# Attention's last value sums in a bank of the scores, and the first MLP unit with its high weights' products first

## The chip, the cores and the metric

The kernel runs on one core of a Trainium2 chip. The metric is the device time of one execution in microseconds (us). TensorE (PE) multiplies and accumulates into the eight banks of PSUM, VectorE (DVE) and ScalarE (ACT) read PSUM and work on SBUF, GpSimd (POOL) works on SBUF alone, and the queue of SyncE (SP) issues the transfers. PEld in the rows is PE's load of the stationary operand, which runs beside its matmuls.

## What is computed

A masked attention over 2 batches, 8 heads, 768 positions and 64 channels is followed by two MLPs over the 1536 tokens. The mask lets a query see the keys with its own hash bucket.

```python
scores = scale * np.matmul(q, k.transpose(0, 1, 3, 2))
scores = np.where(mask, scores, -1000000000.0)
attn = np.exp(scores - np.max(scores, axis=-1, keepdims=True))
attn = attn / (np.sum(attn, axis=-1, keepdims=True) + 1e-09)
x = np.matmul(attn, v)                       # then (1536, 512)

g = x @ w_gate                               # 512 x 1536
x = (g * sigmoid(g) * (x @ w_val)) @ w_out   # 1536 x 512

h = x @ w_in                                 # 512 x 1024
solu = h * softmax(h)
out = (layernorm(solu) * g_ln) @ w_out2      # 1024 x 512
```

## The kernel before

Each number is split into a high and a low part of reduced precision, and each product of two is done as three matmuls: high by high, high by low, low by high. The high part is a cast, the low part a subtraction.

**Attention** goes by slots: 128 queries of one head against its 768 keys. Three slots make a quarter, and a pair of heads has four. For each slot PE writes the scores `s` (two buffers of two PSUM banks, pool `ps_s`), DVE takes the maxima, ACT the exponentials, PE turns them (`transposes`, L535), ACT casts the high part `eh` (L544) and DVE subtracts the low part `el` (L548). `values` (L551 on) then multiplies a whole quarter's `eh` and `el` with the values, in three parts of four matmuls, and adds them up in one PSUM tile `av` of 128 x 384; its pool `ps_a` has one buffer, bank 6. `results` (L602 on) takes `av` out. For the last two quarters it does so without a transfer: ACT copies the lower half of the tile (L624), DVE adds the upper half to it (L626), and only then may the next quarter's `values` overwrite the bank. `spread` (L593 on) turns the reciprocals of the row sums with three PE transposes into the tile `pp` (pool `ps_p`, one buffer), and DVE multiplies the result `xf` by it (L649; for the last quarter L629). POOL, or ACT and DVE for the last quarter, then split `xf` into `xh` and `xl`.

**The first MLP** goes by units. A unit (`hidden`, L930 on) takes 128 of the 1536 hidden columns and 512 tokens: 12 matmuls give the gate `h0` and 12 the value `h1`. Their pool `ps_h` has two buffers for each, and takes over the four banks of `ps_s`: the first `h0` lies in bank 0, the first half of the scores' first buffer, and the first `h1` in bank 2. Then come Silu on ACT (L945), the product on DVE (L946) and the split (L948, L951). Three units share one set of weights.

**Weights** come as 64-bit numbers. DVE turns each piece into 32-bit floats in six steps (`to_float32`, L47 to L64), one ACT cast and one DVE subtraction split it (L913, L915). The first unit's weights are ready as floats before; ACT casts their high part (L841) and POOL subtracts the low part (L842).

**The order** on each engine is fixed when the program is built. Inside each of the two stages it is the code's. Where the stages meet, a scheduler with a cost model interleaves the rows of both: it put two matmuls of the first MLP unit ahead of the last quarter's `values`, and others between its parts.

Of the kernel before, what the change touches and what calls it, by code (L numbers as in the profile page):

```python
# [9 lines left out]
F32 = mybir.dt.float32  # L10
# [10 lines left out]
P = 128  # L21
# [46 lines left out]
def hash_attention_then_two_mlps(  # L68
# [16 lines left out]
    nc = tc.nc  # L85
# [6 lines left out]
    HALF = S // 2  # L92
    CH = C // 2
    NP = H // 2
    KD = DM // P
    KF = DFF // P
    KF2 = DFF2 // P
    BLK = 512
# [12 lines left out]
    xh = xpool.tile([P, KD, NT], R32, tag="h", name="xh")  # L111
    xl = xpool.tile([P, KD, NT], R32, tag="l", name="xl")
# [93 lines left out]
    with at:  # L206
# [4 lines left out]
        ps_s = at.enter_context(tc.tile_pool(name="ps_s", bufs=2, space=PSUM))  # L211
# [246 lines left out]
        for top in tops:  # L458
            nc.vector.memset(top, 1.0)
        s_of, nm_of, e_of, t_of, eh_of, el_of, av_of, total_of, r_of, rs_of, x_of = (  # L460
            {} for _ in range(11)
        )
        NQ = NSLOT // CH

        def quarter(h):


            p, l = divmod(h, 4)
            return (p, l // 2, l % 2) if p == 0 else (p, l % 2, l // 2)
# [83 lines left out]
        def values(h, part):  # L553


            if not 0 <= h < NQ:
                return
            p, j, n = quarter(h)
            if part == 0:
                av_of[h] = ps_a.tile([P, HALF], F32, tag="av", name="av")  # L560
            av = av_of[h]
            vj = parts[p, "v"][:, j].rearrange("p c t d -> p c (t d)")
            for c in range(2 * part, 2 * part + 2):
                low = (av[0:D], vj[:, c, 0:D], el_of[h][:, c, :])
                if c == C - 1:
                    nc.tensor.matmul(*low, start=False, stop=False)
                nc.tensor.matmul(  # L567
                    av, vj[:, c], eh_of[h][:, c, :], start=c == 0, stop=c == C - 1
                )
                if c < C - 1:  # L570
                    nc.tensor.matmul(*low, start=False, stop=False)  # L571
# [171 lines left out]
        with tc.manual_schedule():  # L743
# [7 lines left out]
            for i in range(NSLOT + 9):  # L751
                p, l = divmod(i, SLOTS)
                h, part = divmod(i - 5, CH)
# [25 lines left out]
                if part == 2 and h == NQ - 1:  # L779
                    spread(*quarter(h)[::2])  # L780
                values(h, part)
                go(work)
                if i == 2:
# [30 lines left out]
    with ExitStack() as m1:  # L814
        def pool(name, bufs, **kw):
            return m1.enter_context(
                tc.tile_pool(name=name, bufs=bufs, reuse_waits="tile", **kw)
            )
# [4 lines left out]
        ps_h = pool("ps_h", 2, space=PSUM)  # L823
# [10 lines left out]
        def weights1(f):  # L834
            hi, lo = halves(ws)
            w1_of[f] = [x.rearrange("p n (k f) -> p n k f", k=KD) for x in (hi, lo)]
            return hi, lo

        hi, lo = weights1(0)
# [89 lines left out]

        def hidden(f, blk):  # L930
            hi, lo = w1_of[f]
            ps = []
            for n in range(2):
                p = ps_h.tile([P, BLK], F32, tag=f"h{n}", name=f"h{n}")
                for kk in range(KD):
                    for a, x in ((hi, xh), (hi, xl), (lo, xh)):
                        nc.tensor.matmul(  # L937
                            p, a[:, n, kk, :], x[:, kk, blk * BLK:(blk + 1) * BLK],
                            start=kk == 0 and a is hi and x is xh,
                            stop=kk == KD - 1 and a is lo,  # L940
                        )
                ps.append(p)
            yield
            sg = sg_.tile([P, BLK], F32, tag="sg", name="sg")
            nc.scalar.activation(sg, ps[0], AF.Silu)  # L945
            nc.vector.tensor_mul(sg, ps[1], sg)  # L946
            ah = ap_.tile([P, BLK], R32, tag="ah", name="ah")
            nc.scalar.copy(ah, sg)  # L948
            yield
            al = ap_.tile([P, BLK], R32, tag="al", name="al")  # L950
            nc.vector.tensor_sub(al, sg, ah.bitcast(F32))  # L951
            act[f, blk] = ah, al
# [38 lines left out]
        with tc.manual_schedule():  # L991
# [5 lines left out]
            for t in range(TH):  # L997
                for unit in range((FT + 1) * NBLK):
                    f, blk = divmod(unit, NBLK)
                    reached = (t, unit)  # L1000
                    if t == TH - 1 and unit == FT * NBLK:

                        yh = xpool.tile([P, KD, NT], R32, tag="h", name="yh")
                        yl = xpool.tile([P, KD, NT], R32, tag="l", name="yl")
                    work = hidden(t * FT + f, blk) if f < FT else summed(t, blk)
                    go(work)
                    if f < FT:

                        go(stream)
                        go(before)  # L1010
                        for _ in range(3):
                            if next(stream, None) == "copied":
                                break
                        go(work)
                        before = work
                        continue

                    go(before)
                    before = lows(blk - 1) if t == TH - 1 and blk else iter(())
                    for d in range(KD):  # L1020
                        if blk and t == TH - 1:
                            go(before)
                        elif d != 1:
                            go(stream)
                        go(work)
    with ExitStack() as m2:
# [7 lines left out]
        ps_h = pool("ps_h2", 2, space=PSUM)  # L1034
# [135 lines left out]
```

## Time and profile before

| | us |
|---|---|
| median of 3 runs (lowest, highest) | 703.41 (701.28, 703.53) |
| the profiled execution's own time | 704.01 |
| its span, from the first to the last instruction | 702.2 |
| PE busy in the span | 692.0 |
| DVE busy | 557.0 |
| ACT busy | 339.3 |
| POOL busy | 150.6 |

Times in the rows count from the start of the span. The rows of one engine's timeline show start, duration, line, tiles and shape; in square brackets stands the idle time before a row and what ended it. A matmul's duration is longer than the time until the next can start, so how fast PE goes is read from the distance between starts.

### The profile page before, as it was taken

How to read it: one execution, taken by the hardware profiler on the slowest of the kernel's cores; microseconds unless marked ns; L12 is line 12 of the kernel's file. 1: busy time of each engine (PE TensorE's matmuls, PEld its weight loads, DVE VectorE, ACT ScalarE, POOL GpSimd, SP SyncE). 2: the span in 40 equal slices, each digit the busy share in tenths (PEclk: the TensorE clock that was granted, in tenths of full speed). 3: DMA queues.
4: the chain of work that ended last, by engine and by line, in shares of the span. 5: the costliest groups of instructions: out<-in, count | busy, mean ns of one | idle time of the engine just before them, and what ended most of it. 6: DMA issues, size and time to landing. Idle time of an engine off the chain costs nothing.

```text
span 702.2 us, 10083 instructions
## 1 busy us (share of the span) xinstructions
PE 692.0 (99%) x3683; PEld 592.8 (84%) x3683; DVE 557.0 (79%) x974; ACT 339.3 (48%) x676; POOL 150.6 (21%) x156
## 2 busy tenths in 40 slices
PE   8999999999999999999999999999999999999997
PEld 5899999999999978888888888888888888888886
DVE  6799999999989988767786887977988886655461
ACT  4888989889898954432213122032133522222222
POOL 7346666556634260000000000000000000000000
PEclk7899999999999999999999999999999999999999
DMA  7654746547161403231323131131321000000001
GB/s 209 150 137 126 177 114 161 127 116 176 39 156 43 134 12 120 65 116 61 106 74 118 62 119 62 60 121 60 91 95 56 1 15 16 31 15 16 31 15 46
DMA packets 36177, 60.59 MB, mean 86 GB/s; under 512 B 4984, under 2 KB 26552, under 8 KB 35616
## 3 DMA queue, kind: packets, MB, share of 16 engines
q1 hardware_dynamic: 36128, 59.95, 29.6%
q8 instruction: 29, 0.48, 0.3%
q14 instruction: 20, 0.16, 0.1%
HBM read 36.71 MB, written 3.15 MB: 57 GB/s over the span
## 4 chain that ended last, share of the span: by engine, by line
PE 93%; DVE 2%; issue 2%; ACT 2%; DMA 1%; POOL 0%; SPq 0%; ACTq 0%; POOLq 0%; DVEq 0%
PE h L937 28%; PE h L1050 10%; PE s L484 9%; PE t L535 8%; PE y L963 5%; PE y L964 5%; PE y L962 5%; PE av L567 4%; PE av L571 4%; PE o L1101 3%; PE o L1103 3%; PE o L1102 3%; PE pp L443 2%; PE pp L405 2%; PE t L1088 1%
## 5 line engine op out<-in xcount | busy, mean ns | idle before, releaser
L937 PE MATMUL h<-xh,hi 128*128 128x512 f32 x288 | 112.2, 389 | 0.1
L937 PE MATMUL h<-xl,hi 128*128 128x512 f32 x288 | 112.1, 389 | 0.0
L937 PE MATMUL h<-xh,lo 128*128 128x512 f32 x288 | 112.1, 389 | 0.0
L548 DVE TENSOR_TENSOR el<-t,eh 128x384 fp32r<-128x384 f32 x192 | 97.8, 550 | 9.2 <-ACT eh L544 6.8
L520 ACT ACTIVATE e<-s,nm 128x768 f32<-128x768 f32 x96 | 97.8, 1019 | 5.9 <-DVE nm L504 2.7
L1076 POOL TENSOR_TENSOR w<-w,half 128x1 f32<-128x1 f32 x12 | 6.6, 551 | 416.2 <-DVE w L1075 311.0
L544 ACT CAST eh<-t 128x384 fp32r<-128x384 f32 x192 | 84.1, 494 | 21.8 <-PE t L535 20.5
L495 DVE TENSOR_REDUCE top<-s 128x1 f32<-128x768 f32 x96 | 90.6, 944 | 3.7 <-PE s L484 3.5
L535 PE MATMUL t<-idr,e 128*128 128x128 f32 x576 | 81.0, 276 | 0.4 <-DVE el L548 0.3
L535 PEld LDWEIGHTS t<-idr,e 128*128 128x128 f32 x576 | 68.5, 141 | 9.7 <-DVE el L548 4.0
L567 PE MATMUL av<-eh,vs 128*128 128x384 f32 x192 | 66.2, 345 | 1.4 <-DVE xf L626 1.4
L937 PEld LDWEIGHTS h<-xh,hi 128*128 128x128 f32 x288 | 54.1, 188 | 11.5 <-ACT hi L841 0.3
L937 PEld LDWEIGHTS h<-xl,hi 128*128 128x128 f32 x288 | 54.1, 188 | 11.3
L937 PEld LDWEIGHTS h<-xh,lo 128*128 128x128 f32 x288 | 54.1, 188 | 11.1
L948 ACT CAST ah<-sg 128x512 fp32r<-128x512 f32 x36 | 22.4, 623 | 74.7 <-DVE sg L946 74.7
L484 PE MATMUL s<-ka,qa 128*128 128x384 f32 x192 | 56.5, 376 | 0.0
L963 PE MATMUL y<-al,hi 128*128 128x512 f32 x144 | 56.1, 389 | 0.0
L962 PE MATMUL y<-ah,hi 128*128 128x512 f32 x144 | 56.1, 389 | 0.0
L964 PE MATMUL y<-ah,lo 128*128 128x512 f32 x144 | 56.0, 389 | 0.0
L946 DVE TENSOR_TENSOR sg<-h,sg 128x512 f32<-128x512 f32 x36 | 24.8, 689 | 37.7 <-PE h L937 22.1
L571 PE MATMUL av<-el,vs 128*64 128x384 f32 x160 | 54.0, 338 | 0.0
L913 ACT CAST hi<-wf 128x1024 fp32r<-128x1024 f32 x17 | 17.9, 1050 | 69.8 <-DVE wf L64 69.8
(195 smaller groups left out, 1427.3 us busy)
## 6 DMA issues: line engine op xcount, KB each, us to landing
raw<-in_moe_w_out_dram SPq DMA_DIRECT2D x10, 1024.0 KB
raw<-in_moe_w_gate_dram SPq DMA_DIRECT2D x12, 512.0 KB
raw<-in_moe_w_val_dram SPq DMA_DIRECT2D x12, 512.0 KB
ka<-kt SPq DMA_DIRECT2D x30, 192.0 KB
raw<-in_moe_w_in_dram SPq DMA_DIRECT2D x4, 1024.0 KB
v<-in_v_dram SPq DMA_DIRECT2D x8, 384.0 KB
kb<-kt SPq DMA_DIRECT2D x15, 192.0 KB
qb<-qa SPq DMA_DIRECT2D x15, 192.0 KB
```

Of the source, the lines that this page charges most:

```text
L484: nc.tensor.matmul(s[:, n, :HALF], a[:, rows], m[:, n * HALF:(n + 1) * HALF], start=first, stop=not first,)
L495: nc.vector.tensor_reduce(top[:, 1:2], s_of[i][:, :, :HALF], AX.XY, ALU.max, negate=True)
L520: nc.scalar.activation(e, s_of.pop(i)[:, :, :HALF], AF.Exp, bias=nm[:, 1:2], scale=nm[:, 0:1], accum_out=total_of[p, n][:, j, c:c + 1],)
L535: nc.tensor.transpose(t[:, m, :], e_of[i][:, g, m * P:(m + 1) * P], idf)
L544: nc.scalar.copy(half_tile(eh_of, i, g), t_of[i, g])
L548: last_of[i] = nc.vector.tensor_sub(half_tile(el_of, i, g), t_of.pop((i, g)), half_tile(eh_of, i, g).bitcast(F32),)
L567: nc.tensor.matmul(av, vj[:, c], eh_of[h][:, c, :], start=c == 0, stop=c == C - 1)
L571: nc.tensor.matmul(*low, start=False, stop=False)
L937: nc.tensor.matmul(p, a[:, n, kk, :], x[:, kk, blk * BLK:(blk + 1) * BLK], start=kk == 0 and a is hi and x is xh, stop=kk == KD - 1 and a ...
L962: nc.tensor.matmul(p, hi[:, cols], ah, start=f == t * FT, stop=False)
L963: nc.tensor.matmul(p, hi[:, cols], al, start=False, stop=False)
L964: nc.tensor.matmul(p, lo[:, cols], ah, start=False, stop=f == (t + 1) * FT - 1)
```

## The change

`values` takes the tile of the last quarter (h = NQ - 1) from the scores' pool `ps_s` and uses the first 384 columns of its first bank. By the alternation of the two buffers that is bank 0. All other quarters stay in `ps_a`. Nothing else in `values` or `results` is touched; `results` copies and adds from the tile that it is given.

`hidden` writes its 24 matmuls from a list. For the very first unit the list is sorted so that the 16 products with high weights (`hi` by `xh` and by `xl`, first for `h0`, then for `h1`) stand ahead of the 8 with low weights. All other units keep their order. Number, shape and operands of all instructions are the same.

```diff
@@ values
-            if part == 0:
+            if part == 0 and h == NQ - 1:
+                av_of[h] = ps_s.tile([P, 2, 512], F32, tag="s", name="s")[:, 0, :HALF]
+            elif part == 0:
                 av_of[h] = ps_a.tile([P, HALF], F32, tag="av", name="av")
@@ hidden
-            ps = []
-            for n in range(2):
-                p = ps_h.tile([P, BLK], F32, tag=f"h{n}", name=f"h{n}")
-                for kk in range(KD):
-                    for a, x in ((hi, xh), (hi, xl), (lo, xh)):
-                        nc.tensor.matmul(
-                            p, a[:, n, kk, :], x[:, kk, blk * BLK:(blk + 1) * BLK],
...
+            ps = [ps_h.tile([P, BLK], F32, tag=f"h{n}", name=f"h{n}") for n in range(2)]
+            order = [
+                (n, kk, a, x)
+                for n in range(2) for kk in range(KD)
+                for a, x in ((hi, xh), (hi, xl), (lo, xh))
+            ]
+            if f == blk == 0:
+                order.sort(key=lambda o: o[2] is lo)
+            for n, kk, a, x in order:
+                nc.tensor.matmul(
+                    ps[n], a[:, n, kk, :], x[:, kk, blk * BLK:(blk + 1) * BLK],
...
```

The scheduler orders the seam between the stages anew. On PE, before, from the first `spread` of the seam on (`pp_3884` is its tile, `av_3888` the last quarter's, `h0_3988` the first unit's):

```order
L600 MATMUL pp_3884<-idr_95,wide_3857 128x128 [waits Pool_49]
L600 MATMUL pp_3884<-idr_95,wide_3857 128x128 x2
L937 MATMUL h0_3988<-xh_61,hi1_3973 128x512 [waits Activation_49]
L937 MATMUL h0_3988<-xl_62,hi1_3973 128x512
L567 MATMUL av_3888<-eh_3820,vs_3440 128x384 [waits DVE_49]
L571 MATMUL av_3888<-el_3821,vs_3440 64x384
```

The wait for DVE is the one for L626 of the quarter before, which reads the one bank of `av`. Six more `values` rows follow, then ten rows of `h0` and two of `h1`, the second `spread` with the last four `values`, and the rest of the unit. The same place on PE in the changed program, up to the first row of the unit (lines from 560 on stand 3 higher, the unit's matmul at L945; `s_3888` is the last quarter's tile):

```order
L603 MATMUL pp_3884<-idr_95,wide_3857 128x128 x2
L570 MATMUL s_3888<-eh_3820,vs_3440 128x384 [waits Activation_49]
L574 MATMUL s_3888<-el_3821,vs_3440 64x384 [waits DVE_49]
...
L603 MATMUL pp_3903<-idr_95,wide_3894 128x128 [waits DVE_49,Pool_49]
L603 MATMUL pp_3903<-idr_95,wide_3894 128x128 x2
L570 MATMUL s_3888<-eh_3820,vs_3440 128x384
L574 MATMUL s_3888<-el_3821,vs_3440 64x384
L569 MATMUL s_3888<-el_3821,vs_3440 64x384
L570 MATMUL s_3888<-eh_3820,vs_3440 128x384
L945 MATMUL h0_3988<-xh_61,hi1_3973 128x512 [waits DVE_49]
```

Left out are six more `values` rows. All twelve `values` matmuls and the second `spread` now stand ahead of the whole unit, and the unit's first row waits for DVE. On DVE, before, the rows from the two that follow the second last quarter on (`xf_3880<-av_3888` reads the last quarter):

```order
L626 TENSOR_TENSOR xf_3880<-av_3834,low_3881 64x384 [waits Activation_49]
L649 TENSOR_TENSOR xf_3721<-xf_3721,pp_3884 128x384 [waits DMAHW7_49,PE_49,Pool_49]
L53 TENSOR_SCALAR wf_3986<-wf_3986 128x1024 [waits DVE_49]
L57 SCALAR_TENSOR_TENSOR wf_3986<-raw_3981,wf_3986 128x1024 [waits DVE_49]
L62 TENSOR_SCALAR raw_3981<-raw_3981 128x1024 [waits DVE_49]
L626 TENSOR_TENSOR xf_3880<-av_3888,low_3881 64x384 [waits Activation_49]
L629 TENSOR_TENSOR xf_3880<-xf_3880,pp_3903 128x384 [waits DVE_49]
```

And in the changed program (`s_3888` in the place of `av_3888`):

```order
L629 TENSOR_TENSOR xf_3880<-av_3834,low_3881 64x384 [waits Activation_49]
L652 TENSOR_TENSOR xf_3721<-xf_3721,pp_3884 128x384 [waits DMAHW7_49,PE_49,Pool_49]
L53 TENSOR_SCALAR wf_3986<-wf_3986 128x1024 [waits DVE_49]
L57 SCALAR_TENSOR_TENSOR wf_3986<-raw_3981,wf_3986 128x1024 [waits DVE_49]
L629 TENSOR_TENSOR xf_3880<-s_3888,low_3881 64x384 [waits Activation_49]
L62 TENSOR_SCALAR raw_3981<-raw_3981 128x1024 [waits DVE_49]
```

The last quarter's addition moved one place up, from behind L62 to behind L57. On ACT the cast of `xh` (L630) moved ahead of the Silu's table load. POOL's order is the same. Around the end of the first MLP a few rows of PE, DVE and ACT trade places, and on SP the small transfer of `g_ln` goes ahead of one weight transfer.

## Rows read from the trace of the kernel before

**Rows 1.** Page, part 1: busy us, share of the span, instructions.

```profile
PE 692.0 (99%) x3683; PEld 592.8 (84%) x3683; DVE 557.0 (79%) x974; ACT 339.3 (48%) x676; POOL 150.6 (21%) x156
```

**Rows 2.** Busy us and instructions of each engine in stretches, with the granted clock.

```profile
core 0: us, PE busy (x) PEld busy (x) DVE busy (x) ACT busy (x) POOL busy (x), PEclk, DMA share, GB/s
...
255.00:257.00 2.00, 0.58 (x4) 0.29 (x3) 1.97 (x4) 0.47 (x1) 2.00 (x3) 1.00 0.00 0
...
265.00:600.00 335.00, 335.00 (x1487) 276.99 (x1486) 267.11 (x375) 94.02 (x143) 2.22 (x4) 1.00 0.22 74
```

**Rows 3.** Timeline of PE where the stages meet.

```profile
start us, us, engine line op out<-in xcount [idle before <-releaser]
...
253.97 0.49 PE L600 MATMUL pp<-idr,wide 128*128 128x128 f32 x3
254.52 0.50 PE L937 MATMUL h<-xh,hi 128*128 128x512 f32 x1
254.86 0.40 PE L937 MATMUL h<-xl,hi 128*128 128x512 f32 x1
256.67 0.44 PE L567 MATMUL av<-eh,vs 128*128 128x384 f32 x1 [1.42 <-DVE xf L626]
...
258.18 0.39 PE L937 MATMUL h<-xh,lo 128*128 128x512 f32 x1
...
260.93 0.49 PE L600 MATMUL pp<-idr,wide 128*128 128x128 f32 x3
261.18 0.42 PE L567 MATMUL av<-eh,vs 128*128 128x384 f32 x1
...
261.79 0.34 PE L567 MATMUL av<-eh,vs 128*128 128x384 f32 x1
261.96 0.40 PE L937 MATMUL h<-xh,lo 128*128 128x512 f32 x1
...
264.27 0.39 PE L937 MATMUL h<-xh,hi 128*128 128x512 f32 x1
```

**Rows 4.** Timeline of DVE in the same stretch.

```profile
253.66 0.98 DVE L548 TENSOR_TENSOR el<-t,eh 128x384 fp32r<-128x384 f32 x2
...
256.07 0.54 DVE L626 TENSOR_TENSOR xf<-av,low 64x384 f32<-64x384 f32 x1
256.54 0.53 DVE L649 TENSOR_TENSOR xf<-xf,pp 128x384 f32<-128x384 f32 x1
257.00 1.30 DVE L53 TENSOR_SCALAR wf<-wf 128x1024 int32<-128x1024 int32 x1
258.34 2.20 DVE L57 SCALAR_TENSOR_TENSOR wf<-raw,wf 128x1024 int32<-128x1024 int32 x1
...
262.67 0.55 DVE L626 TENSOR_TENSOR xf<-av,low 64x384 f32<-64x384 f32 x1 [0.89 <-ACT low L624]
```

**Rows 5.** Timeline of ACT: the copy of the last quarter.

```profile
262.16 0.47 ACT L624 COPY low<-av 64x384 f32<-64x384 f32 x1 [6.67 <-PE av L567]
```

**Rows 6.** Timeline of POOL in the same stretch.

```profile
254.59 1.92 POOL L589 TENSOR_TENSOR wide<-one,r 128x192 f32<-128x192 f32 x2 [1.10 <-PE pp L600]
256.48 2.98 POOL L842 TENSOR_TENSOR lo<-w1f,hi 128x512 fp32r<-128x512 f32 x2
259.43 1.80 POOL L652 TENSOR_TENSOR xh<-xf,one 128x384 fp32r<-128x384 f32 x1
```

**Rows 7.** Stretches again: early ones in which the granted clock changed.

```profile
5.00:8.00 3.00, 1.97 (x13) 1.30 (x12) 1.28 (x2) 2.79 (x4) 2.78 (x11) 1.00 0.70 191
8.00:9.00 1.00, 1.00 (x3) 0.58 (x3) 0.00 (x0) 0.97 (x3) 0.94 (x1) 0.57 1.04 386
9.00:21.00 12.00, 11.06 (x39) 8.11 (x38) 8.04 (x10) 4.01 (x10) 11.56 (x9) 0.50 0.73 209
21.00:22.00 1.00, 1.00 (x6) 1.00 (x5) 0.96 (x3) 0.84 (x3) 0.00 (x0) 0.60 0.11 15
```

**Rows 8.** Timeline of PE: 512-column matmuls early on, and the ones behind them.

```profile
6.12 0.47 PE L355 MATMUL pp<-kt,hash_k 128*128 128x512 f32 x1 [0.48 <-ACT kt L321]
6.42 0.28 PE L355 MATMUL av<-kt,hash_k 128*128 128x256 f32 x1
7.24 0.49 PE L355 MATMUL pp<-kt,hash_first 64*128 64x512 f32 x1 [0.54 <-POOL hash_first L193]
...
14.88 0.80 PE L355 MATMUL pp<-kt,hash_k 128*128 128x512 f32 x1 [0.94 <-DVE qb L379]
15.48 0.43 PE L355 MATMUL av<-kt,hash_k 128*128 128x256 f32 x1
```

**Rows 9.** Two DVE lines over the whole span: duration ns min/median/max, first and last start.

```profile
L53 DVE TENSOR_SCALAR wf<-wf x25: 679/693/1304, 257.0 to 544.8; 128x1024 int32<-128x1024 int32 x25
...
L57 DVE SCALAR_TENSOR_TENSOR wf<-raw,wf x25: 1209/1217/2201, 258.3 to 546.6; 128x1024 int32<-128x1024 int32 x25
```

More of the change, by code (lines that the diff above doesn't have):

```diff
@@ L931, in hidden @@
             hi, lo = w1_of[f]
-            ps = []
-            for n in range(2):
-                p = ps_h.tile([P, BLK], F32, tag=f"h{n}", name=f"h{n}")
-                for kk in range(KD):
-                    for a, x in ((hi, xh), (hi, xl), (lo, xh)):
-                        nc.tensor.matmul(
-                            p, a[:, n, kk, :], x[:, kk, blk * BLK:(blk + 1) * BLK],
[L939 to L942, printed above, removed]
+            ps = [ps_h.tile([P, BLK], F32, tag=f"h{n}", name=f"h{n}") for n in range(2)]
[9 more added lines that the diff above has]
+                    ps[n], a[:, n, kk, :], x[:, kk, blk * BLK:(blk + 1) * BLK],
+                    start=kk == 0 and a is hi and x is xh,
+                    stop=kk == KD - 1 and a is lo,
+                )
             yield
```

## The prediction, made before the run

> **What bounds the kernel now.** I read the shares first: PE is busy for 692.0 of 702.2 us [rows 1], so only what lets PE idle, or slows it, can move the time. Next come the stretches, of which two matter [rows 2]. From 265 to 600 us PE is busy for 335.00 of 335 us: whatever time the seam between attention and the first MLP gains or loses is carried to the end, since nothing behind it waits that could absorb it, and the other engines' work there hangs on PE's own units and moves with them. From 255 to 257 us PE is busy for only 0.58 of 2 us: that is the seam. The timeline of PE shows the gap [rows 3]: after two matmuls of the first MLP unit the next row, the first of the last quarter's values, starts at 256.67 after 1.42 us of idle time, released by L626 on DVE, which reads the quarter before out of the single `av` bank.
>
> **The wait that is removed.** With a bank of its own the last quarter needs only its operands. The first spread starts at 253.97, and a spread holds PE for 0.25 (260.93 to 261.18 [rows 3]), so its values start at 254.22. Their last `el` is being made from 253.66, two pieces in 0.98 us [rows 4]; the first piece is there at about 254.2, the second at 254.64, and the second is wanted only by the eighth matmul. Eight value matmuls take 258.18 - 256.67 = 1.51 us [rows 3], so they are done at 255.73. Before, the same point was reached at 258.18, with two unit matmuls done in between (254.52 to 255.09, if the second takes 0.23).
>
> **What is late next.** Two waits, both on DVE, which the old order had hidden.
>
> First, the second spread writes the one `pp` buffer and so waits for L649, which ends at 256.54 + 0.53 = 257.07 [rows 4]. The step from DVE's end to PE's start took 256.67 - (256.07 + 0.54) = 0.06 us [rows 3, 4]. So the spread starts at 257.13, and PE idles from 255.73: 1.40 us. Before, the spread came at 260.93 and waited for nothing. POOL's `wide`, which it also needs, is there at 254.59 + 1.92 = 256.51 [rows 6], in time.
>
> Second, spread and four value matmuls take 261.96 - 260.93 = 1.03 us, so PE is through with attention at 258.16; the last value matmul starts 0.86 us into that (261.79), at 257.99. The unit's first row must then wait, because `h0` lies in the same bank 0: ACT's copy starts 0.37 us after the start of that matmul (261.79 to 262.16 [rows 3, 5]), at 258.36, and is done at 258.83. DVE, however, is not free. Its addition L626 stands behind L53 and L57 in the new order, and L57 ends at 258.34 + 2.20 = 260.54 [rows 4]. None of these DVE and POOL rows waits for anything that the change moves, so I take their times as they stand. L626 starts a little before its forerunner's end (L649 did by 0.07), at 260.47, takes 0.54 and lets PE go at 261.07. It takes no longer beside POOL: it took 0.54 with POOL at work (256.07) and 0.55 with POOL nearly done (262.67). PE idles from 258.16 to 261.07: 2.91 us.
>
> **The unit itself.** From 261.07 PE does 24 matmuls. After a wait the first holds PE for 0.34 (254.52 to 254.86), and ten of the same kind took 264.27 - 261.96 = 2.31, or 0.23 each [rows 3]; together 0.34 + 23 x 0.23 = 5.63, so the second unit starts at 266.70. Before it started at 264.27. **The seam costs 2.4 us at full clock.** The two parts of it agree: idle time of 1.40 + 2.91 = 4.31 us in place of 1.58 (255.09 to 256.67) and 0.30 (254.22 to 254.52). The sorting of the high weights' products costs and gains nothing: it was to keep PE from waiting for POOL's low weights, but L842 ends at 256.48 + 2.98 = 259.46 [rows 6], before the unit can begin at all. Its bounds are 0 and 0.
>
> The rest I cost at nothing. The table load on ACT moves behind the `xh` cast, but Silu needs `h0`, which comes later than both. The rows that trade places at the end of the first MLP lie where PE never waited (335.00 of 335), with the same DVE work in front. The `g_ln` transfer goes in front of a weight transfer that is wanted many units later. If one of these covers were gone, a DVE step of 1.2 us (L57's median [rows 9]) would be the likely price; the range has room for it.
>
> **The clock.** The trace shows that PE's clock can fall in a thin stretch. From 5 to 8 us PE was busy for 1.97 of 3 us, with gaps of 0.48 and 0.54; then the granted clock fell from 1.00 to 0.50 (2.4 to 1.2 GHz) and stayed there past 21 us [rows 7, 8]. In the gap at 255 us, 0.58 busy of 2, it stayed at 1.00 [rows 2]. The new seam is thinner than either: from 255.73 to 261.07, 5.3 us, PE works for 1.03. I take it that the clock falls. What it costs then: at the lower level a 512-column matmul holds PE twice as long (14.88 to 15.48 against 6.12 to 6.42: 0.60 and 0.30 [rows 8]), so half of the time that the unit's stream spends there is lost. How long a dense stream stays there no row shows. One end is 0. The other is the longest that PE worked without a pause before the clock came back, from 14.88 to within 21 to 22 us, at most 6.7 us (60% mean clock in that slice puts the rise at 21.8), a loss of 3.4; with the pauses, from 8 us on, it was 13 us, a loss of 6.5, but in that stretch PE was held up again and again. The unit's stream has no pauses, so I go by the nearer row and take the middle of 0 and 3.4: 1.7 us.
>
> The Trainium skill, page "TensorE: Matmul & The Clock Gate", section "Why this matters for your kernels", warns of PE idle gaps between bursts of matmuls from a certain length on; each of the two gaps worked out here is shorter. By that rule the clock would stay, and the time would be that of the first rival below. The fall at 8 us, after gaps that are shorter still, is why I give it the smaller chance.
>
> **The sum.** 2.4 + 1.7 = 4.1 us. Against the profiled execution's own 704.01 us (span 702.2) that gives 708.1; the median of the three runs is 0.6 lower, 703.41, and against it I forecast **707.5 us**.
>
> **The rivals.**
>
> - The clock stays up: the seam costs its 2.4 us alone, 705.8. For it: the clock stood through 1.42 us of idle time. Against it: two gaps close together, the second twice that long.
> - DVE is not held up, and the time is not slower beyond what can be told: this one ends on the other side. L53 and L57 took 1.30 and 2.20 us where their medians over 25 are 0.69 and 1.22 [rows 4, 9], with POOL at work beside them [rows 6]. If that did not come back, L57 would end at 257.00 + 0.69 + 0.04 + 1.22 = 258.95, L626 at 259.4, the unit would start at 259.5 and the seam would cost 0.8 us: 704.2, with too short a gap for the clock to fall. The balance point is 258.6: a unit that starts by then costs nothing. Against it: POOL's rows are the same in the new order, and nothing releases them later.
> - The bank does not bind: the unit starts right behind the values at 258.16, and 5.63 us later the second unit at 263.79, 0.5 us earlier than before: 702.9. The order speaks against it, since the unit's first row has a wait for DVE. Even so it would be a gain too small to tell.
>
> **How the numbers follow.** This kernel's measurement can tell about 0.3%, or 2.1 us, from no change. Forecast (clock falls) 0.64, clock stays 0.22, DVE free 0.08, bank free 0.03, anything else 0.03. The forecast's own range goes from 2.4 + 0.5 to 2.4 + 3.4 us, 706.3 to 709.2. For 8 in 10 I reach down into the rival of the clock, with 1 us for the spread of the runs (701.28 to 703.53 for one kernel): 704.6 to 709.4. Slower by over 0.3%: nearly all of the forecast and a little over half of the clock's rival, whose 2.4 us lie close to the bound, 0.76. Within: 0.21. Faster: 0.03.
>
> **What would show it.** In the profile of the changed kernel: no wait ahead of the first value matmul at about 254.2; an idle time of about 1.2 to 1.4 us ahead of the second spread, ended by DVE's product (L652 there); one of about 2.7 to 2.9 us ahead of the unit's first row at about 261, ended by DVE's addition (L629 there), with L57 at about 2.2 us just before it; a granted clock under 1.00 somewhere from 259 to 268 us and starts of the unit's matmuls some 0.43 us apart there; from then on PE busy without a gap up to 600 us. If the unit starts before 260, the DVE step is wrong; if the clock stays at 1.00, its step is; if PE idles anywhere from 270 to 600, the view that the rest just moves along is.

## The result, and the profile after

The changed kernel is slower by about half a per cent: a median of 707.5 us (705.76 to 709.47, 6 runs) against 703.77 us (701.28 to 705.11, 6 runs) of the kernel before, a ratio of 1.0055 with a 95% interval of 1.0032 to 1.0078. Its profiled execution took 705.76 us, with a span of 704.0.

The page's first part of the changed kernel answers to [rows 1]: busy us, share of the span, instructions.

```profile
PE 689.7 (98%) x3683; PEld 590.3 (84%) x3683; DVE 554.9 (79%) x974; ACT 339.9 (48%) x676; POOL 150.6 (21%) x156
```

The instruction counts are the same to the last one; PE's busy time is even 2.3 us less. That comes from ahead of the place that the change touches: up to the first spread of the seam PE is busy for 245.7 us, and for 249.5 in the kernel before. The stretches show a clock that differs there (busy us and count of each engine, granted clock, DMA share, GB/s; compare [rows 2, 7]):

```profile
core 0: us, PE busy (x) PEld busy (x) DVE busy (x) ACT busy (x) POOL busy (x), PEclk, DMA share, GB/s
...
9.00:21.00 12.00, 10.63 (x60) 7.59 (x60) 10.49 (x18) 7.73 (x18) 11.62 (x9) 1.00 0.71 213
...
255.00:259.00 4.00, 1.37 (x8) 1.00 (x9) 3.90 (x5) 0.48 (x1) 3.92 (x4) 0.99 0.00 0
259.00:262.00 3.00, 3.00 (x8) 2.33 (x9) 1.54 (x3) 1.79 (x2) 1.40 (x1) 0.50 0.00 0
...
266.00:600.00 334.00, 334.00 (x1483) 276.01 (x1482) 265.57 (x368) 94.13 (x143) 2.23 (x4) 1.00 0.22 74
```

Three things are to be seen here. From 9 to 21 us the granted clock is 1.00, where it was 0.50 in the execution of before that was profiled [rows 7]. From 255 to 259 us PE is busy for 1.37 of 4 us, and from 259 to 262 us the granted clock is 0.50 (1.2 GHz). And from 266 to 600 us PE is busy for 334.00 of 334 us, as it was before: nothing behind the seam waits.

Since the early clock differs between the two executions, the two spans can't be set against each other. What can is the **seam**: from the start of the first spread of `pp` (the L600 row at 253.97 in [rows 3], L603 in the changed kernel) to the first matmul of the second MLP unit. The timeline of PE in the changed kernel (start, duration, engine, line, operation, tiles, and in brackets the idle time before and what ended it):

```profile
251.72 0.49 PE L603 MATMUL pp<-idr,wide 128*128 128x128 f32 x3
251.97 0.42 PE L570 MATMUL s<-eh,vs 128*128 128x384 f32 x1
...
253.27 0.34 PE L574 MATMUL s<-el,vs 128*64 128x384 f32 x1
255.39 0.52 PE L603 MATMUL pp<-idr,wide 128*128 128x128 f32 x3 [1.78 <-DVE xf L652]
...
256.27 0.34 PE L570 MATMUL s<-eh,vs 128*128 128x384 f32 x1
258.85 0.75 PE L945 MATMUL h<-xh,hi 128*128 128x512 f32 x1 [2.24 <-DVE xf L629]
259.40 0.63 PE L945 MATMUL h<-xl,hi 128*128 128x512 f32 x1
259.83 0.63 PE L945 MATMUL h<-xh,hi 128*128 128x512 f32 x1
...
266.01 0.39 PE L945 MATMUL h<-xh,hi 128*128 128x512 f32 x1
```

The seam takes 266.01 - 251.72 = 14.29 us; before it took 264.27 - 253.97 = 10.30 [rows 3]. The difference is 3.99 us. What follows it, from the second unit's start to the end of the span, takes 704.0 - 266.01 = 437.99 us, and took 702.2 - 264.27 = 437.93. What comes ahead of it is 2.25 us shorter in this execution (251.72 against 253.97), and that alone keeps the two spans only 1.8 us apart.

The values of the last quarter start at once (251.97), and the wait of 1.42 us in [rows 3] is gone. Two waits stand in its place, both ended by DVE, and behind the second the first eight of the unit's matmuls start some 0.43 us apart instead of 0.23. The chain that ended last, in the same stretch, says what they consist of (start, duration, piece):

```profile
252.47 0.95 DVE wf L47
...
253.51 0.73 issue
254.24 0.54 DVE xf L629
254.78 0.46 DVE xf L652
255.24 0.76 DVE wf L53
...
256.03 2.18 DVE wf L57
...
258.24 0.56 DVE xf L629
...
258.85 8.23 PE h L945 x28
```

From 252.47 to 258.85 the chain runs through DVE alone (the "issue" of 0.73 us lies within the 0.88 that L51 takes from 253.44). L53 and L57 convert a weight, which can come later, as an experiment below shows; the addition L629 stands behind them.

### The profile page after: what moved, and what is told of

Its sections match the earlier page's. It is cut to its first block, busy times and chain, and to the rows that moved or that the text cites. A ratio compares the mean times of both kernels' runs of the same rounds, so it can differ in the third digit from the quotient of the medians.

```text
span 704.0 us, 10084 instructions
## 1 busy us (share of the span) xinstructions
PE 689.7 (98%) x3683; PEld 590.3 (84%) x3683; DVE 554.9 (79%) x974; ACT 339.9 (48%) x676; POOL 150.6 (21%) x156
## 4 chain that ended last, share of the span: by engine, by line
PE 91%; DVE 2%; ACT 2%; issue 2%; DMA 1%; POOL 1%; SPq 0%; ACTq 0%; POOLq 0%; DVEq 0%
PE h L945 28%; PE h L1057 10%; PE s L484 9%; PE t L535 8%; PE y L969 5%; PE y L970 5%; PE y L971 5%; PE av L570 4%; PE av L574 4%; PE o L1108 3%; PE o L1110 3%; PE o L1109 3%; PE pp L443 2%; PE pp L405 2%; PE t L1095 1%
## 5 line engine op out<-in xcount | busy, mean ns | idle before, releaser
L945 PE MATMUL h<-xh,hi 128*128 128x512 f32 x288 | 113.1, 393 | 2.2 <-DVE xf L629 2.2
L945 PE MATMUL h<-xl,hi 128*128 128x512 f32 x288 | 112.9, 392 | 0.0
L945 PE MATMUL h<-xh,lo 128*128 128x512 f32 x288 | 110.9, 389 | 0.0
L945 PEld LDWEIGHTS h<-xh,hi 128*128 128x128 f32 x288 | 54.7, 190 | 14.0 <-DVE xf L629 2.6
L945 PEld LDWEIGHTS h<-xl,hi 128*128 128x128 f32 x288 | 54.6, 190 | 11.3
L570 PE MATMUL av<-eh,vs 128*128 128x384 f32 x186 | 64.0, 344 | 0.0
L945 PEld LDWEIGHTS h<-xh,lo 128*128 128x128 f32 x288 | 54.1, 188 | 11.3
L574 PE MATMUL av<-el,vs 128*64 128x384 f32 x155 | 52.3, 337 | 0.0
```

The costliest lines, as they stand in the source:

```text
L570: nc.tensor.matmul(av, vj[:, c], eh_of[h][:, c, :], start=c == 0, stop=c == C - 1)
L945: nc.tensor.matmul(ps[n], a[:, n, kk, :], x[:, kk, blk * BLK:(blk + 1) * BLK], start=kk == 0 and a is hi and x is xh, stop=kk == KD - 1 an ...
```

## The experiments

All eight are compared by the seam, as above, in one profiled execution of each; times are medians, and each ratio is to the kernel before on the same chip (703.77 us, 6 runs, for the changed kernel; 703.59 us, 24 and 23 runs, for the others).

| kernel | seam us | less before's | time us (runs) | ratio to before, 95% interval |
|---|---|---|---|---|
| before | 10.30 | | | |
| after | 14.29 | +3.99 | 707.5 (6) | 1.0055, 1.0032 to 1.0078 |
| bank only | 15.29 | +4.99 | 707.85 (4) | 1.0057, 1.0042 to 1.0073 |
| sorting only | 8.60 | -1.70 | 700.83 (7) | 0.9963, 0.9949 to 0.9977 |
| DVE free | 10.70 | +0.40 | 704.01 (10) | 1.0005, 0.9992 to 1.0018 |
| PE kept busy | 12.72 | +2.42 | 705.67 (11) | 1.0025, 1.0015 to 1.0034 |
| bank of `t` | 8.33 | -1.97 | 701.1 (7) | 0.9964, 0.995 to 0.9978 |
| bank of `t`, no sorting | 10.03 | -0.27 | 703.09 (10) | 0.9995, 0.9985 to 1.0004 |
| other half of the tile | 14.29 | +3.99 | 705.07 (1) | |
| before, gap filled | 10.32 | +0.02 | 703.43 (11) | 0.9993, 0.9983 to 1.0004 |

**The bank alone.** The sorting is taken out of the changed kernel. Theory: the cost is the bank's. Rival: it is the sorted order's.

```diff
-            if f == blk == 0:
-                order.sort(key=lambda o: o[2] is lo)
```

> The bank alone, without the sorting. The seam is counted from the start of the first spread to the start of the second unit's first matmul: 10.30 us before, 14.29 us in the change. My theory (the unit waits for DVE's late reading of bank 0, and then the clock is down): as the change, since the low weights are ready before the unit can begin; seam 14.0 to 14.6 us, time about 3.8 us over before. Rival (the sorted order is what costs): seam near 10.3 us and no time lost.

The timeline of PE of this kernel:

```profile
257.10 0.52 PE L603 MATMUL pp<-idr,wide 128*128 128x128 f32 x3 [1.77 <-DVE xf L652]
260.56 0.80 PE L942 MATMUL h<-xh,hi 128*128 128x512 f32 x1 [2.23 <-DVE xf L629]
...
265.42 0.63 PE L942 MATMUL h<-xh,lo 128*128 128x512 f32 x1
265.84 0.52 PE L942 MATMUL h<-xh,hi 128*128 128x512 f32 x1
```

Both waits are there, with the same releasers and to 0.01 us the same lengths. The bank brings them, whatever the unit's order. The seam is 1.0 us longer than in the changed kernel, and longer than the 14.0 to 14.6 us expected, because twelve matmuls held PE for 0.42 us or more each, where the changed kernel had eight of 0.41 or more; the granted clock was 0.50 from 260 to 265 us. One execution of each doesn't tell whether the order or chance did that; the medians are 0.35 us apart, within the spread.

**The sorting alone.** The last quarter goes back to the `av` bank, the sorting stays.

```diff
-            if part == 0 and h == NQ - 1:
-                av_of[h] = ps_s.tile([P, 2, 512], F32, tag="s", name="s")[:, 0, :HALF]
-            elif part == 0:
+            if part == 0:
```

> The sorting alone, the last quarter's values back in the single bank. My theory: the 16 products with high weights stand ahead of the last values and fill the 1.42 us in which PE waited for L626; the order has nothing that waits behind them; seam 8.6 to 9.0 us in place of 10.30, time 1.3 to 1.7 us under before, the clock at full speed. Rival (the sorted order is what costs): seam over 10.3 us, time at or over before.

The timeline of PE:

```profile
251.28 0.49 PE L600 MATMUL pp<-idr,wide 128*128 128x128 f32 x3
251.82 0.50 PE L942 MATMUL h<-xh,hi 128*128 128x512 f32 x1
...
255.59 0.33 PE L567 MATMUL av<-eh,vs 128*128 128x384 f32 x1
...
259.88 0.40 PE L942 MATMUL h<-xh,hi 128*128 128x512 f32 x1
```

Sixteen products of the unit's high weights (from 251.82 to 255.59) now fill the time in which PE used to wait for the `av` bank; no row of the seam has a wait in brackets any more. The seam is 1.70 us shorter than before's, of which 1.58 was PE's empty slot (255.09 to 256.67, by the prediction's count from [rows 3]). The kernel is faster than before by 2.76 us, 1.06 more than its seam and more than the 1.3 to 1.7 us expected; the interval, 1.6 to 3.6 us, still holds 1.70.

**DVE free.** Of the conversion that stood in DVE's queue only L47 stays ahead of the first unit; the other steps come behind it. (They are done later, not left out.)

```diff
-                        go(stream)
+                        if t or unit:
+                            go(stream)
                         go(before)
-                        for _ in range(3):
+                        for _ in range(3 if t or unit > 1 else 5 * unit):
```

> The change, but the first unit takes no conversion steps on DVE (L51 to L62 of the first weight piece come one unit later), so that nothing but L47 stands in front of the two additions. My theory: the unit starts about 2.1 us earlier in the seam than in the change, with gaps of about 1.0 and 1.3 us in place of 1.78 and 2.24; seam 10.4 to 10.8 us if the clock then stays up, 12.0 to 12.5 if it falls all the same; time 0.2 to 0.6 over before, or 1.8 to 2.2 over. Rival (what holds the unit is the chain from the last values through ACT and DVE itself, not DVE's other work): the gap ahead of the unit stays at 2.2 us or more, time as the change.

The timeline of PE, then that of POOL:

```profile
256.77 0.52 PE L603 MATMUL pp<-idr,wide 128*128 128x128 f32 x3 [0.85 <-DVE xf L652]
...
259.14 0.49 PE L945 MATMUL h<-xh,hi 128*128 128x512 f32 x1 [1.15 <-DVE xf L629]
259.47 0.39 PE L945 MATMUL h<-xl,hi 128*128 128x512 f32 x1
259.70 0.40 PE L945 MATMUL h<-xh,hi 128*128 128x512 f32 x1
```

```profile
256.03 2.49 POOL L845 TENSOR_TENSOR lo<-w1f,hi 128x512 fp32r<-128x512 f32 x2
258.48 0.82 POOL L655 TENSOR_TENSOR xh<-xf,one 128x384 fp32r<-128x384 f32 x1
```

Without L51, L53 and L57 in front of DVE's additions both waits halve, the matmuls start 0.23 us apart from the second one on (the granted clock was 1.00 from 255 to 262 us), and the loss shrinks from 3.99 to 0.40 us of seam. The time can't be told from before's. So it is those conversions, through their place in DVE's queue, that make the new bank dear.

**PE kept busy.** Into both waits go matmuls into a `t` tile that nobody reads: seven ahead of the second spread, twelve behind the last values. The waits stay what they are for DVE; only the clock should change.

```diff
                 if part == 2 and h == NQ - 1:
+                    t = ps_t.tile([P, 512], F32, tag="t", name="t")
+                    for _ in range(7):
+                        nc.tensor.matmul(t[:, :HALF], idr, eh_of[h][:, 0, :], start=True, stop=True)
                     spread(*quarter(h)[::2])
                 values(h, part)
+                if part == 2 and h == NQ - 1:
+                    t = ps_t.tile([P, 512], F32, tag="t", name="t")
+                    for _ in range(12):
+                        nc.tensor.matmul(t[:, :HALF], idr, eh_of[h][:, 0, :], start=True, stop=True)
```

> The change, with idle matmuls put into the two gaps: 7 of 128 x 384 ahead of the second spread and 12 behind the last values, into a bank of the transposes that nothing reads afterwards. My theory (the clock is a term of its own): the waits stay where they are, the clock stays at 1.00, the unit's matmuls start 0.23 us apart from the first on; seam about 12.7 us (14.29 less 8 matmuls x 0.2 us), time about 2.2 to 2.6 over before and 1.2 to 1.7 under the change. Rival (the clock falls anyway, or its price is not in the time): seam 14 us or more, time as the change.

The timeline of PE:

```profile
254.77 1.38 PE L785 MATMUL t<-eh,idr 128*128 128x384 f32 x7
256.70 0.52 PE L603 MATMUL pp<-idr,wide 128*128 128x128 f32 x3 [0.55 <-DVE xf L652]
...
257.75 2.24 PE L791 MATMUL t<-eh,idr 128*128 128x384 f32 x12
260.18 0.50 PE L952 MATMUL h<-xh,hi 128*128 128x512 f32 x1 [0.19 <-DVE xf L629]
260.52 0.40 PE L952 MATMUL h<-xl,hi 128*128 128x512 f32 x1
...
265.75 0.39 PE L952 MATMUL h<-xh,hi 128*128 128x512 f32 x1
```

The stretch with both waits and the first of the unit (columns as above; the granted clock is the third number from the end):

```profile
255.00:262.00 7.00, 6.26 (x34) 5.28 (x33) 6.32 (x9) 1.11 (x3) 6.65 (x5) 1.00 0.01 2
```

The second spread and the unit are let go by the same rows at the same distance from the first spread (3.66 and 7.14 us; 3.67 and 7.13 in the changed kernel), but the unit's 24 matmuls take 265.75 - 260.18 = 5.57 us where they took 266.01 - 258.85 = 7.16. Nineteen useless matmuls make the kernel 1.8 us faster than the changed one by the medians (1.65 if each is set against its own kernel before), 1.57 by the seam; over the kernel before it is 2.1 us, a little less than the 2.2 to 2.6 expected. That is the price of the clock, apart from the waits.

**A bank that the unit's tiles don't wait for.** The changed kernel with its last quarter in a bank of `ps_t`.

```diff
-                av_of[h] = ps_s.tile([P, 2, 512], F32, tag="s", name="s")[:, 0, :HALF]
+                av_of[h] = ps_t.tile([P, 512], F32, tag="t", name="t")[:, :HALF]
```

> The change with the last quarter's values in a bank of the transposes in place of one of the scores; the sorting stays. My theory (the cost comes from the choice of a tile that the first unit needs next): the unit's first row no longer waits for DVE, the scheduler puts its 16 high products in front of the second spread, and both gaps go; seam 8.2 to 8.6 us (10.30 before, 14.29 in the change, 8.60 with the sorting alone), time 1.7 to 2.8 under before, as the sorting alone or up to 0.4 better. Rival (a bank of its own for the last quarter costs by itself, wherever it lies): seam over 10.3 us, time not under before.

The timeline of PE:

```profile
253.53 0.49 PE L603 MATMUL pp<-idr,wide 128*128 128x128 f32 x3
...
255.13 0.40 PE L945 MATMUL h<-xh,hi 128*128 128x512 f32 x1
...
259.89 0.49 PE L603 MATMUL pp<-idr,wide 128*128 128x128 f32 x3
...
261.86 0.39 PE L945 MATMUL h<-xh,hi 128*128 128x512 f32 x1
```

Sixteen high products, and four low ones, now stand ahead of the second spread, which waits for nothing. The seam is 1.97 us shorter than before's. This kernel and the one with the sorting alone are faster than both the kernel before and the changed one; between the two of them (701.1 and 700.83) the runs don't decide.

**The same bank without the sorting.**

```diff
-            if f == blk == 0:
-                order.sort(key=lambda o: o[2] is lo)
```

> As the run before, without the sorting. My theory: PE reaches the first low weights' product about 2.4 us after the first spread's start and waits there for POOL's first subtraction (L842), which ended 3.8 us after that spread's start before; so one gap of 1.0 to 1.6 us, ended by POOL, seam 9.4 to 10.1 us, time 0.2 to 1.0 under before. Rival (the sorting is worth nothing where the bank is free): seam 8.2 to 8.6 us.

The timeline of PE:

```profile
255.41 0.40 PE L942 MATMUL h<-xl,hi 128*128 128x512 f32 x1
...
257.40 0.49 PE L942 MATMUL h<-xh,lo 128*128 128x512 f32 x1 [1.42 <-POOL lo L845]
```

In the old order the unit's third matmul reads the low weights, and PE waits for POOL to make them. The seam is 1.70 us longer than with the sorting: that is what the sorting is worth once the unit may start early. It is the wait that the sorting was written against, and the changed kernel never reaches it.

**The other half of the tile.** The values go into the second bank of the scores' tile instead of the first. Theory, as the prediction had it: `h0` waits because it lies in the same bank as the values, so with the values in bank 1 it would not (the unit's `h1` lies in bank 2). Rival: the wait is for the whole tile.

```diff
-                av_of[h] = ps_s.tile([P, 2, 512], F32, tag="s", name="s")[:, 0, :HALF]
+                av_of[h] = ps_s.tile([P, 2, 512], F32, tag="s", name="s")[:, 1, :HALF]
```

> The change with the values in the second of the two banks of the scores' tile (columns 512 to 895 in place of 0 to 383). The first unit's first tile lies in the first of them. If the wait is for the whole tile's release: as the change, a gap of over 2 us ahead of the unit's first row, seam 14 to 15.5 us. If it is for the bank: no wait there, the unit starts about 1.0 us behind the second spread's start, seam 10.6 to 11.4 us.

The timeline of PE:

```profile
254.73 0.52 PE L603 MATMUL pp<-idr,wide 128*128 128x128 f32 x3 [1.78 <-DVE xf L652]
...
258.19 0.50 PE L945 MATMUL h<-xh,hi 128*128 128x512 f32 x1 [2.23 <-DVE xf L629]
```

Nothing changes: the same waits and, by the seam, the same 14.29 us. The unit's first tile waits until the last reader of the two-bank tile is through, in whichever half the values lie. That it is this tile and not all of the pool `ps_s` is taken from the code, which opens `ps_h` with `reuse_waits="tile"`; no run tries it.

**Before, with its gap filled.** Eight matmuls that nobody reads go into the wait of 1.42 us of the kernel before. It asks whether that gap costs clock as well, which could be the 1.06 us by which the sorting alone gained more than its seam.

```diff
                     spread(*quarter(h)[::2])
+                if part == 0 and h == NQ - 1:
+                    t = ps_t.tile([P, 512], F32, tag="t", name="t")
+                    for _ in range(8):
+                        nc.tensor.matmul(t[:, :HALF], idr, eh_of[h][:, 0, :], start=True, stop=True)
                 values(h, part)
```

> The kernel before with 8 idle matmuls of 128 x 384 in its one gap of 1.42 us. Nothing else moves. If the clock never falls in that gap: seam 10.2 to 10.4 us and the time within 0.4 us of before. If it falls there in some executions of before, which would explain why the sorting alone gave 2.8 us where its seam is 1.7 us shorter: seam the same, time 0.5 to 1.2 us under before.

The timeline of PE:

```profile
256.01 0.44 PE L567 MATMUL av<-eh,vs 128*128 128x384 f32 x1 [0.31 <-DVE xf L626]
```

The seam stays at 10.32 us and the time moves by -0.16 us, within its interval (-1.2 to +0.3). The gap of before cost no clock that the runs can tell. Where the sorting's extra 1.06 us came from stays open; the early clock, below, moves single executions by that much and more.

## Why the prediction came out

The time was forecast at 707.5 us and is 707.5. That it fits to the tenth is luck: 4.1 us over a median of 703.41 were forecast, 3.7 over one of 703.77 measured, and the seam of the profiled execution is 3.99 us longer. The steps, one by one:

- **The wait that is removed**: right. The values start 0.25 us behind the first spread and take 1.48 us, where 1.51 was reckoned.
- **The first new wait**: right in kind and releaser (L652), too small in size. From the end of the values' slot at 253.45 (253.27 and the 0.175 that one of them holds PE) to 255.39 it is 1.94 us, where the prediction had 1.40. The term that failed is DVE's side of it, taken over from the rows of before "as they stand": L652 ended 3.52 us after the first spread's start (254.78 + 0.46 - 251.72), its forerunner 3.10 [rows 4], and the step to PE took 0.15 us (to 255.39), not 0.06. The last section shows the row that grew.
- **The second new wait**: right in kind and releaser (L629 behind L57 of 2.18 us), too large: from 256.44 to 258.85 it is 2.41 us, where 2.91 was reckoned. The same rows make up for the first wait: L57 ends at 258.21, which is 6.49 us after the first spread's start, and ended 6.57 after it before [rows 4]. Together the two waits are 4.35 us; 4.31 was forecast. The sum held since both hang on one queue of DVE whose end moved little; its division did not. That the rows grew and shrank by nearly the same amount was not foreseen: here two errors made up for each other.
- **Why the unit waits**: wrong in the reason given. It is not "because `h0` lies in the same bank 0": with the values in the other bank the wait is the same. It is the release of the whole tile of two banks. The number didn't depend on it.
- **The clock**: right, and nearly in size. The unit took 7.16 us against 5.63 reckoned at the full clock, so 1.53 us; with the waits filled 1.57 us of seam are saved, 1.65 to 1.8 by the medians; the forecast was 1.7. That the size fits is in part luck: it was the middle between 0 and 3.4, and in the one execution of the bank alone the same 24 matmuls took 8.17 us, 2.5 more than reckoned. (The 13 us at the lower clock, which the forecast set aside, come out at 13.7 from the rows, 8.14 to 21.8.) The row was the granted clock of 0.50 from 259 to 262 us behind the two waits, and 1.00 throughout where PE was kept busy.
- **A rule of the Trainium skill**: the Trainium skill, page "TensorE: Matmul & The Clock Gate", section "Why this matters for your kernels", advises against PE-idle gaps between bursts of matmuls that are longer than either of the two here. By it the clock would have stayed. The trace does not agree: it fell behind waits of 1.78 and 2.24 us by the rows, with 1.05 us of work between them, and with the second of them at 1.15 us (DVE free) it stayed. The measurement decides here.
- **The sorting costs and gains nothing**: right in this change (with and without it both waits are there), wrong as a statement on the sorting. Its bounds of 0 and 0 hold only because the tile's wait comes later than POOL's low weights. Where the unit may start early it is worth 1.70 us of seam, in either bank (8.33 against 10.03, 8.60 against 10.30).
- **The rest just moves along**: right, 437.93 us before and 437.99 after; in all ten profiles it lies between 437.9 and 438.0.

The rivals were worked out to times, and three experiments come close to what they suppose. With the clock kept up 705.8 us were reckoned, and 705.67 measured (2.4 and 2.1 us over the kernel before). With DVE not held up 704.2, and 704.01 (0.8 and 0.4 over it). With a bank that doesn't bind 702.9, and 701.1: here the step was short, since it let the first new wait stand, and the scheduler put sixteen of the unit's sorted products there.

So the change traded a wait of 1.42 us that the sorting alone could have filled for a tile on which the unit itself depends. The last quarter was no longer late, but the work that was to cover it could not begin until the last quarter was through.

## What to carry to other kernels

A tile moved into a free bank takes over that bank's later users: before moving it, look who next gets the tile, which engine releases it, and what stands ahead of that release in that engine's queue. An edit that helps alone can lose all of its gain to another beside it; here the sorting alone gained 1.7 us of seam and gained nothing once the bank, which alone cost 5.0, kept its products from starting. Where executions of one kernel differ in a part that the change doesn't touch, compare the stretch that it does touch from one fixed instruction to another, not the spans.

## What the hardware did that was not expected

**DVE and POOL hold each other up, and which of them goes with who starts first by a few hundredths of a microsecond.** DVE's row L47 and POOL's row L592 (L589 before) start within 0.05 us of each other in every profile. The changed kernel, DVE's timeline and then POOL's:

```profile
252.38 1.03 DVE L47 TENSOR_SCALAR wf<-raw 128x1024 int32<-128x1024 int32 x1
...
255.17 0.82 DVE L53 TENSOR_SCALAR wf<-wf 128x1024 int32<-128x1024 int32 x1
```

```profile
252.35 1.42 POOL L592 TENSOR_TENSOR wide<-one,r 128x192 f32<-128x192 f32 x2 [1.03 <-PE pp L603]
253.73 3.39 POOL L845 TENSOR_TENSOR lo<-w1f,hi 128x512 fp32r<-128x512 f32 x2
```

The kernel with the bank of `t`, likewise:

```profile
254.13 0.68 DVE L47 TENSOR_SCALAR wf<-raw 128x1024 int32<-128x1024 int32 x1
...
256.58 1.32 DVE L53 TENSOR_SCALAR wf<-wf 128x1024 int32<-128x1024 int32 x1
```

```profile
254.16 1.94 POOL L592 TENSOR_TENSOR wide<-one,r 128x192 f32<-128x192 f32 x2 [1.09 <-PE pp L603]
```

Where POOL starts 0.03 to 0.05 us ahead (the five kernels with the scores' bank), L592 takes 1.42 us and L47 1.01 to 1.03; where DVE starts 0.02 to 0.03 ahead (the other five, before among them), L47 takes 0.68 or 0.69 and POOL's row 1.92 to 1.94. Later in the queue it turns round: L53, where it runs there, takes 0.82 or 0.83 us in the first case and 1.29 to 1.32 in the second. This is why the first new wait came out longer and the second shorter than forecast. In the kernel with DVE free the same holds the other way: POOL's L845 took 2.49 us in place of 3.39, and L655 0.82 in place of 1.80. The ten profiles show how far back it goes. POOL's row stands 0.62 or 0.63 us behind the first spread in all of them; it is DVE's that comes later, 0.65 to 0.67 us behind it in the first group and 0.59 or 0.60 in the other. An earlier row of DVE (L583, L580 before: the row sums) ends 0.02 or 0.03 us behind POOL's L648 (L645 before) in every one, and POOL waits for the transfer that releases L648 for 1.34 or 1.35 us in the first group, 1.27 or 1.28 in the other. Why the transfer lands later there was not tried.

The Trainium skill, page "SBUF — State Buffer", section "Who interferes with whom", says of the ports that the two engines share: "Issue order, not op shape, decides who blocks." The trace agrees, with 0.32 to 0.35 us on L47 and 0.50 to 0.52 on POOL's row between the two orders; no run changed the order and nothing else. A prediction that takes a duration over from the trace of before takes over that order with it.

**The early clock differs between executions.** From 8 to 22 us the granted clock was 1.00 in three of the ten profiles (the changed kernel, the sorting alone, the other half of the tile), 0.51 to 0.54 in four (before among them) and between 0.67 and 0.88 in three. With it the start of the first spread moved from 251.07, 251.28 and 251.72 us in the first three to between 253.04 and 254.02 in the others. No kernel was profiled twice, but the mean granted clock of the whole span is on record for each execution: over 24 of the kernel before it goes from 0.988 to 1.000, so a clock that is lower in one execution than in the next is not the kernel's doing. Where in the span it was low is known of the profiled ones alone. The times go from 701.38 us (at 1.000) to 705.83 (at 0.988), though not strictly with the clock (704.17 at 1.000). That is more than the change moves, and one pair of profiles taken by their spans would have put it at 1.8 us instead of 4.0.
